# The last group's second channel product: one outer product moved to the end and left untransposed

## The chip, the cores and the metric

One core of a Trainium2 chip runs the kernel. The metric is the device time of one execution in microseconds (us). A profiled execution also gives a trace with a span, from the first to the last instruction. The engines are named as in the profile: PE is TensorE's matmul, PEld its weight load, DVE VectorE, ACT ScalarE, POOL GpSimd, SP the engine that issues most DMAs.

## The reference

Linear attention without softmax for 8 batches and 8 heads, and then an MLP mixer on its output. All is fp32.

```
kv  = einsum('bhsd,bhse->bhde', k, v);  o = einsum('bhsd,bhde->bhse', q, kv)
x   = o / sqrt(mean(o*o) + 1e-6) * g_norm          # to (8, 576, 512)
u   = x + transpose(relu(transpose(x) @ w_tok1) @ w_tok2)
out = u + relu(u @ w_ch1) @ w_ch2                  # w_ch1 512x1536, w_ch2 1536x512
```

The change is in the last line, in the product with `w_ch2` and in the addition to `u`.

## The kernel before

**Stages.** Until about 226 us the kernel computes attention and token mixing and writes `u` to `out` in DRAM. Then come the channel products, for nine units of 512 rows: the first 512 rows of each of the 8 batches, and the last 64 rows of all of them together. Group 0 is one unit; groups 1 to 4 have two units each.

**A channel product of two levels.** In groups 1 to 4 the product is split by a scheme with seven multiplications where a plain 2x2 block product has eight, and each of the seven is split so once more. So the first channel product of a group (`channel1`, L971) has seven outer products of seven inner products, and the second (`channel2`, L1028) as many. An inner product is three matmuls of 128x128 weights with 256 columns, each of which the trace lists as two records. Groups 1 to 4 thus have 98 inner products each.

**Places.** The order is written by hand. Each inner product has a place, and `beside[place]` lists the steps of the other engines that are recorded right behind it (`put`, L867). At the end one loop goes over the places, and so each engine's queue has this order. `outer` (L870) sets the seven inner products of one outer product to the places of `PLACE` (L863): 1, 5, (4 of the outer before), 6, 2, 3, 7, and its own 4 stands two places into the next outer. The very last outer uses `LAST` (L864), so that its 4 is in the last place: 1, 5, (4 of the outer before), 6, 2, 7, 3, 4. In the text "place p" of a channel product counts from its first inner product, so outer i starts at place 7i, and the last place of the last group is 49.

**What an inner product leaves.** The results are in three kinds of PSUM tiles: `ps_a` and `ps_b`, of which there is one each, and `ps_d`, of which there are two. Product 1 goes to `ps_a`, and ACT copies it to `ps_d`, where 6, 7 and 4 are added; 2 is added in `ps_a`; 5 goes to `ps_b`, and 3 is added there. After 5 and 6 a temporary is read (`p5`, `u2`; `read`, L885), and after 2, 3, 7 and 4 a quarter of the result is written. A quarter without `base` is read by an ACT copy (for 2 and 4) or a DVE add with `p5` or `u2` (`join`, L929, for 3 and 7); with `base` all of these reads are DVE adds.

**The second channel product.** The outer order is `ORDER2` (L949): 1, 2, 4, 7, 6, 5, 3. The left operands are sums of blocks of relu(u @ w_ch1), made by DVE: the wide sums of 128x1536 (`A`, `S1` to `S4`) and, for each outer, four steps of 128x768 to the tiles `sv` (`inner`, L1060; `ins[o][0]` to `ins[o][3]`). The weights of an inner product come from DRAM by SP, about seven to twelve places ahead (`fetch_ahead`, L963). The result is transposed by matmul order: weights `w` are stationary and the activations stream. Each result tile `rs[o]` is 128x1024, that is 128 columns by 512 rows of the output.

The four output quarters are: (0,0) = r1 + r2; (1,0) = r4 + r7 + r6 (r6 read with `base` r1); (1,1) = r7 + r5; (0,1) = r5 + r6 + r3, in running sums. The first index is the unit, the second the half of the output columns. A finished quarter is transposed in 32x32 blocks by DVE and added to `u` in DRAM by four accumulating DMAs from POOL (`put_rows`, L1173). In the last group (0,1) is taken another way: `xg`, loaded with `u` of that quarter and transposed ahead, gets r6 and r5, then outer 3's quarters straight from PSUM (`onto`), and is transposed back and stored in pieces (`store_part`, L1178), four stores of 32 KB each from SP, ACT and POOL:

```
(47, [store_part((nc.scalar, nc.sync), 0, (0,))]),
(48, [store_part((nc.sync, nc.scalar), 1, (1,)),
      store_part((nc.gpsimd, nc.sync, nc.gpsimd, nc.scalar), 0, (1,))]),
(49, [store_part((nc.sync, nc.scalar), 1, (0,))])
```

Of the kernel before, what the change touches and what calls it, by code (L numbers as in the profile page):

```python
# [20 lines left out]
def kernel(  # L21
# [33 lines left out]
    P = 128  # L55
# [64 lines left out]
    def dma(o, i, engine=nc.sync):  # L120
        keep(engine.dma_start(o, i))
# [7 lines left out]
    def copy(o, a):  # L129
        keep(nc.scalar.copy(o, a))  # L130

    def matmul(*a, **kw):
        keep(nc.tensor.matmul(*a, **kw))  # L133
# [462 lines left out]
    def units(g):  # L596
        return ((0,), (1, 2), (3, 4), (5, B), (6, 7))[g] if g < NG else (NU, NU)
# [272 lines left out]
    def outer(place, size, mul, to, base=None, act=copy, onto=False, last=False):  # L870

        banks, t = {}, {}
        places = LAST if last else PLACE

        def fit(flat):
            return flat.rearrange("p (n j) -> p n j", j=Q) if size == T else flat.rearrange("p (w t) -> p w t", w=W)
# [60 lines left out]
        put(place + places[7], do(join, 1, 1, "d", "p5"))  # L937
# [12 lines left out]
    order = [(w, g, o) for g in range(1, NG) for w, os in ((1, ORDER1), (2, ORDER2)) for o in os]  # L950
    ws, v_in_parts = {}, {}

    def fetch_w(n, k):
# [74 lines left out]
    def channel2(g, n0):  # L1028
# [3 lines left out]
        def second(i, o):  # L1032
            n = n0 + i
            r = {}

            def mul(p, ps, start, stop):
                v = v_in_parts[g, o](p)
                w = w_part(n, p).rearrange("p (w e) -> p w e", w=W)
                for s in range(W):
                    matmul(ps, lhsT=w[:, s], rhs=v[:, s], start=(start and s == 0), stop=stop,  # L1040
                           skip_group_check=True)
# [12 lines left out]
            return r  # L1054

        rs = {}
        for i, o in enumerate(ORDER2):
            rs[o] = second(i, o)

        def inner(o):  # L1060
# [49 lines left out]
        A, S1, S2, S3, S4 = (halves(f) for f in (make_a21, sum1, sum2, sum3, sum4))  # L1110


        for place, steps in (
                (-3, [ins[1][0]]), (-1, [ins[1][1]]), (1, [ins[1][3]]), (2, [ins[1][2]]),
                (3, [ins[2][0]]), (5, [ins[2][1]]), (6, [ins[4][0]]), (7, [ins[2][2]]),
                (8, [A[0]]), (9, [A[1]]), (10, [ins[2][3]]), (11, [S3[0]]), (12, [S3[1]]),
                (13, [ins[4][1]]), (14, [ins[4][2]]), (15, [S2[0]]), (16, [ins[4][3]]), (17, [ins[7][0]]),
                (19, [ins[7][1]]), (21, [S2[1], ins[7][2]]), (23, [ins[7][3]]), (24, [S1[0]]),
                (25, [ins[6][0]]), (29, [S4[0]]), (27, [ins[6][1]]), (28, [S1[1]]), (30, [ins[6][3]]),
                (31, [ins[6][2]]), (32, [ins[5][0]]), (33, [ins[5][1]]),  # L1120
                (35, [ins[5][2]]), (36, [ins[5][3]]), (38, [S4[1]]), (39, [ins[3][0]]), (41, [ins[3][1]]),
                (43, [ins[3][2]]), (45, [ins[3][3]])):
            put(b + place, *steps)

        def join(i, j, o):
            return do(put_rows, units(g)[i], j, lambda: rs[o][0])
# [5 lines left out]

            return step

        for place, step in ((19, radd(2, 1)), (20, join(0, 0, 2)), (39, radd(7, 6)), (40, radd(4, 7)), (41, join(1, 0, 4))):
            put(b + place, step)
        if g < NG - 1:
            for place, step in ((46, radd(7, 5)), (47, radd(5, 6)), (48, join(1, 1, 7)), (52, radd(3, 5)),
                                (55, join(0, 1, 3))):
                put(b + place, step)  # L1140
            if g == NG - 2:
                put(b + 60, do(fetch_x, g + 1))
                put(b + 79, do(turn, lambda: xg[g + 1]))
        else:
            for place, steps in ((38, [xadd(6)]), (44, [radd(7, 5), join(1, 1, 7)]), (46, [xadd(5)]),
                                 (47, [store_part((nc.scalar, nc.sync), 0, (0,))]),
                                 (48, [store_part((nc.sync, nc.scalar), 1, (1,)),
                                       store_part((nc.gpsimd, nc.sync, nc.gpsimd, nc.scalar), 0, (1,))]),
                                 (49, [store_part((nc.sync, nc.scalar), 1, (0,))])):
                put(b + place, *steps)  # L1150

        for k, place in enumerate((6, 8, 12, 36)):
# [22 lines left out]
        for b, at, to in pieces(u, j):  # L1175
            keep(nc.gpsimd.dma_start(to, t()[ds(b * Q, Q), at].rearrange("p n l j -> p n (l j)"), accum_op=ALU.add))  # L1176

    def store_part(queues, i, leaves):  # L1178
        def step():
            lo = leaves[0] * Q  # L1180
            t = xg[NG - 1][:, ts(i, NQ), leaves[0]]
            turn(lambda: t)
            for b in range(NC):
                dma(out[units(NG - 1)[0], ts(i, T), ds(DH + b * HF + lo, Q)].rearrange("(n i) e -> i n e", i=Q),
                    t[ds(b * Q, Q)], queues[b % len(queues)])

        return step

# [181 lines left out]
    def turn_over():  # L1370
        w2s.close()
        late["vr"] = pool("vr", 1, "right")
        late["sv"] = pool("sv", 2, "right")
        late["s3"] = pool("s3", 1, "right")
        late["xg"] = pool("xg", 1, "right")
        late["r"] = pool("r", 3, "right")

    put(9, turn_over)
# [43 lines left out]
```

## Time and profile before

| what | us |
|---|---|
| three runs, median (lowest to highest) | 785.08 (784.42 to 785.74) |
| the profiled execution, its own time | 784.74 |
| its span | 782.9 |
| PE busy in the span | 762.9 (97%) |
| DVE busy | 643.2 (82%) |
| ACT busy | 271.5 (35%) |
| POOL busy | 113.6 (15%) |
| second channel product of the last group, place 0 | starts at 707.15 |
| its last inner product (place 49) | starts at 772.81 |

The rest of the profiled execution's time, 1.84 us, lies around the span. The profile gives a start and a length for each instruction; a matmul's end is modelled, so that pace on PE is read from start to start. "Idle before" names what an engine waited for. DMAs have an issue on their engine's queue (SPq, ACTq, POOL) and a landing; the profile gives the time between them. In the chain of waits, work is followed back from the last instruction, at each step to what released it.

### The profile page before, as it was taken

The page shows a single profiled execution, that of the slowest core. Times are in us where ns is not written, and L with a number is a line of the kernel's source. Part 1 is how long each engine was busy: PE and PEld are TensorE (multiplying, and loading weights), DVE is VectorE, ACT ScalarE, POOL GpSimd, SP SyncE. Part 2 cuts the span into 40 slices and gives each one's busy share as a digit, 9 for nine tenths or more (in the row PEclk, how much of TensorE's full clock was granted, in tenths as well). Part 3 has the DMA queues.
Part 4 walks back from the last instruction along what each step waited for, and adds up shares of the span by engine and source line. Part 5 has one row for each costly group of instructions (what it writes and reads, how often), then busy time and mean ns, then how long its engine had stood idle before and what let it go on. Part 6 is the DMA issues. An engine that isn't in the chain of part 4 may idle for free.

```text
span 782.9 us, 12672 instructions
## 1 busy us (share of the span) xinstructions
PE 762.9 (97%) x4640; PEld 611.1 (78%) x4640; DVE 643.2 (82%) x957; ACT 271.5 (35%) x534; POOL 113.6 (15%) x130
## 2 busy tenths in 40 slices
PE   6999999999999999999999999999999999999994
PEld 6655555545888888888888888888888888888883
DVE  2867887897766779899978989987989996898995
ACT  2566575664210233511234241133351123424110
POOL 1002020113410000002240002051000236000205
PEclk9999999999999999999999999999999999999998
DMA  9999999999899796689997588899658889655658
GB/s 292 310 322 372 369 365 282 263 237 359 297 280 352 261 290 186 171 266 210 212 232 249 149 251 192 246 200 262 193 167 264 201 192 215 190 156 145 156 131 80
DMA packets 178412, 187.26 MB, mean 239 GB/s; under 512 B 76048, under 2 KB 141072, under 8 KB 178352
## 3 DMA queue, kind: packets, MB, share of 16 engines
q1 hardware_dynamic: 140208, 166.60, 70.4%
q0 software_dynamic: 34880, 18.42, 15.7%
q10 hardware_dynamic: 3264, 1.44, 0.7%
q8 instruction: 37, 0.61, 0.3%
q14 instruction: 23, 0.19, 0.1%
HBM read 137.79 MB, written 48.63 MB: 238 GB/s over the span
## 4 chain that ended last, share of the span: by engine, by line
PE 89%; DMA 5%; DVE 3%; POOL 1%; issue 0%; ACT 0%; ACTq 0%; POOLq 0%; SPq 0%; DVEq 0%
PE ps_d L133 26%; PE ps_b L133 18%; PE ps_a L133 17%; PE ps_u L133 8%; PE ps_h L133 7%; PE ps_v L133 5%; PE ps_c L133 3%; DMA v_in<-in_v_dram 2%; PE ps_w L133 2%; PE ps_kv L133 2%; PE ps_o L133 2%; DMA qR<-in_q_dram 1%; DVE v L124 1%; DMA k_in<-in_k_dram 1%; POOL out_dram L1176 1%; DVE sv L124 1%
## 5 line engine op out<-in xcount | busy, mean ns | idle before, releaser
L133 PE MATMUL ps_d<-ui,w 128*128 128x256 f32 x504 | 118.6, 379 | 0.0
L133 PEld LDWEIGHTS ps_d<-ui,w 128*128 128x128 f32 x504 | 95.8, 190 | 13.0
L130 ACT COPY ps_d<-ps_a 128x768 f32<-128x768 f32 (+1 forms) x56 | 32.0, 572 | 213.0 <-PE ps_a L133 210.0
L124 DVE TENSOR_TENSOR v<-v,v 128x1536 f32<-128x1536 f32 (+2 forms) x70 | 103.3, 1481 | 0.3
L1176 POOL DMA_DIRECT2D out_dram<-us x28 | 31.1, 1816 | 370.9 <-ACT p L130 366.0
L133 PE MATMUL ps_b<-sv,w 128*128 128x256 f32 x336 | 82.4, 381 | 1.4 <-DVE sv L124 1.0
L133 PE MATMUL ps_a<-v,w 128*128 128x256 f32 x336 | 81.7, 379 | 0.0
L133 PEld LDWEIGHTS ps_b<-sv,w 128*128 128x128 f32 x336 | 63.0, 190 | 12.9 <-DVE sv L124 2.8
L133 PEld LDWEIGHTS ps_a<-v,w 128*128 128x128 f32 x336 | 63.8, 190 | 8.7
L133 PE MATMUL ps_h<-x,w_tok 128*128 128x512 f32 (+1 forms) x160 | 65.2, 602 | 0.4 <-DVE x L503 0.4
L133 PE MATMUL ps_d<-v,w 128*128 128x256 f32 x264 | 64.3, 379 | 0.6 <-DVE xg L124 0.6
L133 PE MATMUL ps_u<-h,w_tok 128*128 128x512 f32 (+1 forms) x160 | 64.7, 599 | 0.0
L127 ACT ACTIVATE v<-v 128x768 f32<-128x768 f32 (+1 forms) x54 | 42.6, 822 | 55.1 <-DVE v L124 52.3
L133 PE MATMUL ps_d<-sv,w 128*128 128x256 f32 x240 | 58.3, 379 | 0.0
L1176 POOL DMA_DIRECT2D out_dram<-r x40 | 41.4, 1994 | 105.6 <-ACT p L130 81.6
L133 PEld LDWEIGHTS ps_d<-v,w 128*128 128x128 f32 x264 | 50.1, 190 | 7.7 <-DVE xg L124 1.0
L133 PEld LDWEIGHTS ps_h<-x,w_tok 128*128 128x128 f32 (+1 forms) x160 | 26.2, 189 | 32.0 <-issue 28.0
L133 PEld LDWEIGHTS ps_d<-sv,w 128*128 128x128 f32 x240 | 45.6, 190 | 6.2
L133 PEld LDWEIGHTS ps_u<-h,w_tok 128*128 128x128 f32 (+1 forms) x160 | 25.6, 179 | 31.1 <-issue 26.7
L133 PE MATMUL ps_a<-uT,w 128*128 128x256 f32 x192 | 46.7, 379 | 0.0
L133 PE MATMUL ps_b<-ui,w 128*128 128x256 f32 x168 | 40.8, 379 | 0.0
L133 PEld LDWEIGHTS ps_a<-uT,w 128*128 128x128 f32 x192 | 36.5, 190 | 5.0
(151 smaller groups left out, 1252.6 us busy)
## 6 DMA issues: line engine op xcount, KB each, us to landing
w<-parts SPq DMA_DIRECT2D x168, 384.0 KB, 3.7
w<-parts SPq DMA_DIRECT2D x56, 192.0 KB, 3.7
uT<-blocks SPq DMA_DIRECT2D x36, 256.0 KB, 5.2
k_in<-in_k_dram SPq DMA_DIRECT2D x16, 512.0 KB, 9.0
qT<-in_q_dram SPq DMA_DIRECT2D x8, 1024.0 KB, 9.7
out_dram<-x POOLq DMA_DIRECT2D x16, 512.0 KB, 6.3
v_in<-in_v_dram SPq DMA_DIRECT2D x14, 512.0 KB, 9.4
raw<-in_moe_w_ch_dram SPq DMA_DIRECT2D x8, 768.0 KB, 8.7
```

The lines of the kernel that those rows point to most:

```text
L124: keep(engine.tensor_tensor(out=o, in0=a, in1=b, op=op))
L127: keep(nc.scalar.activation(o, a, AF.Relu))
L130: keep(nc.scalar.copy(o, a))
L133: keep(nc.tensor.matmul(*a, **kw))
L1176: keep(nc.gpsimd.dma_start(to, t()[ds(b * Q, Q), at].rearrange("p n l j -> p n (l j)"), accum_op=ALU.add))
```

## The change

The outer product 2 of the last group's second channel product goes from second to last: the group's outer order becomes 1, 4, 7, 6, 5, 3, 2. Its operands are exchanged, activations stationary and weights streaming, so that its result has the output's rows on the partitions and needs no transpose; each inner product is then six matmuls of 128 columns in place of three of 256. Quarter (0,0) of the last group is put together in another way: r1 alone is copied by ACT to a new tile `xs` (`first_aside`), transposed, and added to `out` by `put_rows`; later the same rows are read back from `out` to `xs` untransposed (`fetch_last`, one DMA of 512 KB on SP, at place 34); outer 2 is added onto them from PSUM, and they are stored in four DMAs of 128 KB (`store_last`). Quarter (0,1) in `xg` is complete at place 44 and stored by a shorter `store_part`, in eight DMAs of 64 KB. The last group has its own list of places for the sums and the `sv` steps (`ends`).

In all groups outer 6 is now read without `base`; r1 is added afterwards in one DVE add of 128x1024 (`radd(6, 1)`, at place 38, in the last group at 31).

```diff
+    END = NG - 1, 2
+    order2 = lambda g: ORDER2 if g < NG - 1 else (1, 4, 7, 6, 5, 3, 2)
...
+                if (g, o) == END:
+                    for t in range(2):
+                        for s in range(W):
+                            matmul(ps[:, ts(t, P)], lhsT=v[:, s, ts(t, P)], rhs=w[:, s],
+                                   start=(start and t == 0 and s == 0), stop=stop, skip_group_check=True)
+                else:
+                    for s in range(W):
+                        matmul(ps, lhsT=w[:, s], rhs=v[:, s], start=(start and s == 0), stop=stop,
+                               skip_group_check=True)
...
-            if g == NG - 1 and o == 3:
-                outer(7 * n, T, mul, lambda i, j: xg[g][:, ts(i, NQ), j], onto=True, last=True)
-            else:
-                outer(7 * n, T, mul, to, o == 6 and (lambda i, j: rs[1][0][:, ts(i, NQ), j]))
+            if (g, o) == END:
+                outer(7 * n, T, mul, lambda i, j: rows_of(xs[0])[:, ts(i, 2), j], onto=True, last=True,
+                      fit=lambda flat: flat.rearrange("p (t b e) -> p t b e", t=2, b=NC))
+            elif g == NG - 1 and o == 3:
+                outer(7 * n, T, mul, lambda i, j: xg[g][:, ts(i, NQ), j], onto=True)
+            else:
+                outer(7 * n, T, mul, to)
...
+        ends = (
+                (-3, [ins[1][0]]), (-1, [ins[1][1]]), (1, [ins[1][3]]), (2, [ins[1][2]]),
+                (3, [A[0], ins[4][0]]), (5, [A[1]]), (6, [ins[4][1]]), (7, [S3[0]]), (8, [S3[1]]),
+                (9, [ins[4][3]]), (10, [ins[4][2], ins[7][0]]), (12, [ins[7][1]]), (14, [S2[0]]), (15, [ins[7][3]]),
+                (16, [ins[7][2]]), (17, [S2[1]]), (18, [ins[6][0]]), (19, [S1[0]]), (20, [ins[6][1]]), (21, [S4[0]]),
+                (22, [ins[6][3]]), (23, [ins[6][2]]), (24, [S1[1]]), (25, [ins[5][0]]), (26, [ins[5][1]]),
+                (27, [S4[1]]), (28, [ins[5][3]]), (29, [ins[5][2]]), (31, [ins[3][0]]), (32, [ins[3][1]]),
+                (33, [ins[3][3]]), (34, [ins[3][2]]), (36, [ins[2][0]]), (37, [ins[2][1]]), (39, [ins[2][2]]),
+                (40, [ins[2][3]]))
...
+        def first_aside():
+            xs[0] = late["xs"].tile([P, 2 * NQ, 2, Q], F32, name="xs")
+            copy(xs[0], rs[1][0])
...
+            for place, *steps in ((11, first_aside), (17, do(put_rows, units(g)[0], 0, lambda: xs[0])), (31, radd(6, 1)),
+                                  (32, radd(7, 6)), (34, fetch_last), (34, radd(4, 7)), (35, join(1, 0, 4)), (36, xadd(6)),
+                                  (38, radd(7, 5)), (39, join(1, 1, 7)), (41, xadd(5)),
+                                  (44, store_part(0)), (46, store_part(1)),
+                                  (48, store_last(0)), (49, store_last(1))):
...
+    def fetch_last():
+        xs[0] = late["xs"].tile([P, J, DH], F32, name="xs")
+        dma(xs[0], last_rows())
+
+    def store_last(i):
+
+        def step():
+            for t, queue in zip((2 * i, 2 * i + 1), (nc.sync, nc.scalar)):
+                dma(last_rows(t, 1), xs[0][:, ts(t, 1)], queue)
```

More of the change, by code (lines that the diff above doesn't have):

```diff
@@ L865, with outer @@
     products, beside = {}, defaultdict(list)
+    END = NG - 1, 2
     def put(place, *steps):
         beside[place] += steps
-    def outer(place, size, mul, to, base=None, act=copy, onto=False, last=False):
+    def outer(place, size, mul, to, base=None, act=copy, onto=False, last=False, fit=None):
         banks, t = {}, {}
         places = LAST if last else PLACE
-        def fit(flat):
-            return flat.rearrange("p (n j) -> p n j", j=Q) if size == T else flat.rearrange("p (w t) -> p w t", w=W)
+        fit = fit or (lambda flat: flat.rearrange("p (n j) -> p n j", j=Q) if size == T else
+                      flat.rearrange("p (w t) -> p w t", w=W))
         def bank(name):
@@ L949 @@
     ORDER1, ORDER2 = (1, 6, 2, 7, 5, 4, 3), (1, 2, 4, 7, 6, 5, 3)
-    order = [(w, g, o) for g in range(1, NG) for w, os in ((1, ORDER1), (2, ORDER2)) for o in os]
+    order2 = lambda g: ORDER2 if g < NG - 1 else (1, 4, 7, 6, 5, 3, 2)
+    order = [(w, g, o) for g in range(1, NG) for w, os in ((1, ORDER1), (2, order2(g))) for o in os]
     ws, v_in_parts = {}, {}
@@ L1038, in mul @@
                 w = w_part(n, p).rearrange("p (w e) -> p w e", w=W)
-                for s in range(W):
-                    matmul(ps, lhsT=w[:, s], rhs=v[:, s], start=(start and s == 0), stop=stop,
-                           skip_group_check=True)
+                if (g, o) == END:
[7 more added lines that the diff above has]
+                               skip_group_check=True)
             def to(i, j):
@@ L1056, in channel2 @@
         rs = {}
-        for i, o in enumerate(ORDER2):
+        for i, o in enumerate(order2(g)):
             rs[o] = second(i, o)
@@ L1110, in channel2 @@
         A, S1, S2, S3, S4 = (halves(f) for f in (make_a21, sum1, sum2, sum3, sum4))
-        for place, steps in (
+        usual = (
                 (-3, [ins[1][0]]), (-1, [ins[1][1]]), (1, [ins[1][3]]), (2, [ins[1][2]]),
@@ L1121, in channel2 @@
                 (35, [ins[5][2]]), (36, [ins[5][3]]), (38, [S4[1]]), (39, [ins[3][0]]), (41, [ins[3][1]]),
-                (43, [ins[3][2]]), (45, [ins[3][3]])):
+                (43, [ins[3][2]]), (45, [ins[3][3]]))
+        ends = (
[7 more added lines that the diff above has]
+                (40, [ins[2][3]]))
+        for place, steps in usual if g < NG - 1 else ends:
             put(b + place, *steps)
@@ L1133, in both @@
             return step
-        for place, step in ((19, radd(2, 1)), (20, join(0, 0, 2)), (39, radd(7, 6)), (40, radd(4, 7)), (41, join(1, 0, 4))):
-            put(b + place, step)
+        def first_aside():
+            xs[0] = late["xs"].tile([P, 2 * NQ, 2, Q], F32, name="xs")
+            copy(xs[0], rs[1][0])
         if g < NG - 1:
-            for place, step in ((46, radd(7, 5)), (47, radd(5, 6)), (48, join(1, 1, 7)), (52, radd(3, 5)),
-                                (55, join(0, 1, 3))):
-                put(b + place, step)
+            for place, *steps in ((19, radd(2, 1)), (20, join(0, 0, 2)), (38, radd(6, 1)), (39, radd(7, 6)), (40, radd(4, 7)),
+                                  (41, join(1, 0, 4)), (46, radd(7, 5)), (47, radd(5, 6)), (48, join(1, 1, 7)),
+                                  (52, radd(3, 5)), (55, join(0, 1, 3))):
+                put(b + place, *steps)
             if g == NG - 2:
@@ L1144, in channel2 @@
         else:
[L1145 to L1149, printed above, removed]
+            for place, *steps in ((11, first_aside), (17, do(put_rows, units(g)[0], 0, lambda: xs[0])), (31, radd(6, 1)),
[3 more added lines that the diff above has]
+                                  (48, store_last(0)), (49, store_last(1))):
                 put(b + place, *steps)
@@ L1176, in put_rows, with store_part @@
             keep(nc.gpsimd.dma_start(to, t()[ds(b * Q, Q), at].rearrange("p n l j -> p n (l j)"), accum_op=ALU.add))
[L1178 removed]
+    def store_part(i):
         def step():
[L1180 to L1181 removed]
+            t = xg[NG - 1][:, ts(i, NQ)]
             turn(lambda: t)
             for b in range(NC):
[L1184 to L1185 removed]
+                dma(out[units(NG - 1)[0], ts(i, T), ds(DH + b * HF, HF)].rearrange("(n i) e -> i n e", i=Q),
+                    t[ds(b * Q, Q)].rearrange("p n l j -> p n (l j)"), nc.scalar if i and b % 2 else nc.sync)
+        return step
+    last_rows = lambda t=0, n=J: out[units(NG - 1)[0], ds(t * P, n * P), :DH].rearrange("(t p) e -> p t e", p=P)
+    rows_of = lambda x: x.rearrange("p t (b l e) -> p t l b e", b=NC, l=2)
+    xs = {}
+    def fetch_last():
[5 more added lines that the diff above has]
+                dma(last_rows(t, 1), xs[0][:, ts(t, 1)], queue)
         return step
@@ L1375, in turn_over @@
         late["xg"] = pool("xg", 1, "right")
+        late["xs"] = pool("xs", 1, "right")
         late["r"] = pool("r", 3, "right")
```

## The prediction

> **What bounds the kernel now.** I read the page first (TensorE busy 97% of the span, DVE 82%, granted clock 0.996), then the chain of waits, then the timeline from 700 us on, and last the rows for single tiles. In the chain of waits the columns are start, length, what.
>
> ```profile
> 345.68 2.59 PE ps_d L133 x12
> 354.75 2.59 PE ps_d L133 x12
> 363.23 1.64 DVE v L124
> 365.20 1.66 DVE v L124
> 367.79 1.56 PE ps_b L133 x6
> 373.24 2.59 PE ps_d L133 x12
> ...
> 718.97 2.59 PE ps_d L133 x12
> 728.30 2.59 PE ps_d L133 x12
> 737.37 2.59 PE ps_d L133 x12
> ```
>
> An outer product (seven inner products, one "place" each) returns every 9.07 us: 1.295 us a place. Two intervals are longer. 354.75 to 373.24 is 18.49, where two periods make 18.13: 0.36 lost, at the ps_b product at 367.79 that waited for DVE. That is place 33 of the second channel product (3 of outer 6), and 482.29 to 500.78 and 609.83 to 628.32 show the same 0.36. 718.97 to 728.30 is 9.33: 0.26 lost at place 12 in the last group.
>
> ```profile
> 766.43 8.72 POOL L1176 DMA_DIRECT2D out_dram<-r  x8 [24.04 <-ACT r L130]
> 768.28 1.46 PE L133 MATMUL ps_d<-v,w 128*128 128x256 f32 x6
> 770.69 1.56 PE L133 MATMUL ps_b<-sv,w 128*128 128x256 f32 x6 [0.95 <-DVE sv L124]
> 772.81 1.56 PE L133 MATMUL ps_d<-v,w 128*128 128x256 f32 x6 [0.56 <-DVE xg L124]
> 773.14 5.50 SPq L121 DMA_DIRECT2D out_dram<-xg  x7
> 773.14 6.11 ACTq L121 DMA_DIRECT2D out_dram<-xg  x7
> 774.41 0.42 DVE L124 TENSOR_TENSOR xg<-ps_d,xg 128x256 f32<-128x256 f32 x1 [0.32 <-PE ps_d L133]
> ```
>
> From start to start the last two products come 770.69 - 769.575 = 1.115 and 772.81 - 771.985 = 0.825 us late: 1.94 us of DVE backlog. After the last product there are still 774.41 to 782.9 = 8.49 us:
>
> ```profile
> 774.40:782.90 8.50, 0.00 (x0) 0.00 (x0) 0.87 (x2) 0.00 (x0) 1.95 (x3) 0.66 0.95 105
> ```
>
> No engine works there; the DMA engines are 95% busy at only 105 GB/s, with sixteen 32 KB stores in rows of 128 B beside eight accumulating DMAs. The last store is issued at 778.94 and lands 2.6 us later; from that landing to the end of the span are 1.35 us.
>
> ```profile
> L121 ACTq DMA_DIRECT2D out_dram<-xg x1: 322/322/322, 778.9 to 778.9; - x1
> DMA to landing us min/median/max: 2.6/2.9/3.1
> ```
>
> So the end is set by TensorE's places, DVE's backlog on the last two, and a tail of small stores.
>
> **What the Trainium skill says.** "TensorE: Matmul & The Clock Gate", section "Back-to-back issue gap": the spacing of a stream of weight loads and matmuls is set by both, about 81 ns for bf16 with 128 columns, more than the columns alone would take. This kernel is fp32 and its trace has the shape itself, 112 ns (below), so the trace is used. "DMA: Bandwidth & Descriptors", section "Anatomy of one DMA — SWDGE (gpsimd) path": a DMA has about 2.0 us of fixed cost, mostly the write receipt. The trace agrees: 2.6 us for 32 KB, 2.8 us for 512 KB. The same page, "Specifications": below 512 B a row isn't moved at line rate. The trace agrees with 105 GB/s in the tail against 393 GB/s and more in slices around 260 us, where the rows are of 768 B to 3 KB.
>
> **The change part by part.**
>
> *a. Groups 1 to 3, outer 6 read without base.* Four DVE adds from PSUM (0.34 us each from start to start) become ACT copies (0.37; ACT is busy 35%), and one SBUF add of 128x1024 comes at place 38 (1.13 from start to start): DVE has 0.23 us less per group. What counts is that the p5 add (492.33 in group 2) stood in front of the sv that place 33 waits for. That sv ended at 495.28 and TensorE started at 495.33, when it could have at 493.78 + 1.295 = 495.075: 0.26 late, and 0.10 to refill. 0.33 us of relief covers this with 0.07 to spare. -0.36 x 3 = **-1.08**; bounds -1.1 and 0. The new add at 38 comes after more than it costs (1.36) has gone from the places before it.
>
> *b. Last group, place 12.* In the kernel before DVE came from the read at 715.19 to the sv for this product over four sv steps and two wide sums, and TensorE started at 722.88 in place of 722.69: 0.19 late and 0.07 to refill. In the new order there are two sv steps and three wide sums: 1.67 for 2 x 0.87 and 0.10 of a dependence, 0.17 sooner. It is a near thing: **-0.20**, bounds -0.26 and +0.1.
>
> *c. The untransposed product.* Each of the seven inner products of the last outer becomes six matmuls 128x128 in place of three 128x256: 12 records for 6. The nearest row is ps_o in the attention, also fp32, 128x128, with new weights for each matmul:
>
> ```profile
> 29.39 1.95 PE L133 MATMUL ps_o<-kvp,qT 128*128 128x128 f32 x16
> 31.18 1.88 PE L133 MATMUL ps_h<-x,w_tok 128*128 128x512 f32 x4
> L133 PEld LDWEIGHTS ps_o<-kvp,qT x56: 186/192/192, 18.9 to 34.5; 128*128 128x128 f32 x56
> ```
>
> (31.18 - 29.39) / 16 = 0.112 us a record, although a load is listed with 0.19: the loads overlap. 12 x 0.112 - 1.295 = 0.049, seven times: **+0.34**. Bounds: 0 (columns alone), and +7.1 if each load of 0.192 stood alone.
>
> *d. DVE's backlog.* The late steps (the last sv of outer 3, the wide add and the transposes between them) are no longer beside the last outer: outer 3's sv is made at places 31 to 34 and the last outer's at 36 to 40. Both late products lose their wait: -1.94. Another comes: place 43 (product 5 of the last outer) writes ps_b, of which there is one, and must wait for the DVE add that reads outer 3's join from it (place 40). From the last read that TensorE releases (outer 5's second join, place 34, readable 0.27 after its end) DVE has in a row: three PSUM reads of 256 (0.34), two SBUF adds of 256 (0.33), four sv steps of 768 (0.87), three adds of 1024 (1.13) and two transposes (1.16), 0.10 for one dependent pair and 0.08 for the last one's end: 1.02 + 0.66 + 3.48 + 3.39 + 2.32 + 0.18 = 11.05. TensorE gets from that release to place 43 in seven places less 0.27 plus one product of 1.344: 9.065 - 0.27 + 1.344 = 10.14. The wait is 0.91, with refill 1.0; bounds 0.4 and 2.5 (0.12 more for each of the thirteen steps). After it DVE has only six joins of 0.42, one add and two transposes for 9 us, so nothing is late again. -1.94 + 1.0 = **-0.94**.
>
> *e. The tail.* The column half that is transposed is now stored from places 44 and 46 in eight DMAs of 64 KB, rows of 256 B, about 6 and 3 us before the last product ends. The rest ends as: last product readable; one DVE add, 0.43; two DMAs of 128 KB in rows of 1 KB, one on SP and one on ACT, 0.03 to issue, 2.8 to land (the 512 KB store of group 0 took 2.8; the last pair is 256 KB, and I take no less because the pair before is still under way); 1.35 to close. 4.6 against 8.49: **-3.89**; the landing between 2.3 (192 KB of weights at 756.8) and 5.0 (POOL's stores of xg).
>
> *Queues.* The join of (0,0) moves from place 20 to 17, and the copy for it is 1 us on ACT. Its four DMAs on POOL were issued from 738.1 and landed by 747.3 (9.3 us); now about 731 to 741. The read-back is on SP behind the weights of place 33, at about 750, so SP finds them landed and the weights behind it (places 35 and 38, used at 47 and 49) aren't held. It is 512 KB; loads of that size took 9.0 us when crowded, so it is there by 759 for a first use at 766. The joins of (1,0) and (1,1) go to POOL at about 755 and 762 in place of 766 to 772; four take 9.3, so the last lands at 771.5, before the stores do. No cost.
>
> Sum: -1.08 - 0.20 + 0.34 - 0.94 - 3.89 = -5.77. The profiled execution took 784.74 (span 782.9 and 1.84 around it) and would take 779.0; the median of the three runs is 0.34 higher: 785.08 - 5.77 = **779.3 us**.
>
> **The rivals.**
>
> *The stores still drain.* The accumulates of (1,1), the xg stores and the xs stores meet between 767 and 775. If the last pair lands 2.3 us later (5.1, where POOL's stores of xg, issued at 774.4 and 775.0, took a median of 5.0), the time is 781.6. For it: small rows still fill the engines; a store waits for the landing of the eighth SP or ACT DMA before it, which can pass the delay on. Against: half as many packets as before, and started 5 us earlier. 0.12.
>
> *DVE later than summed.* Place 43 takes every delay of DVE one for one. If the wait is 2.5 us in place of 1.0, 780.8. For it: DVE is busy 96% from 761.8 to 774.4 (12.12 of 12.60). Against: such a sum over the sixteen DVE steps from 756.83 in the kernel before gives 13.85 us, so 770.68, and the sv for place 48 ended at 770.64. 0.12.
>
> *Slower: weight loads set the pace of the untransposed product.* 84 records at 0.192 are +7.1 in place of +0.34: 779.3 - 0.34 + 7.1 = 786.1. It decides from 0.112 + 5.77 / 84 = 0.181 us a record. For it: loads are listed with 0.19, twice as many for the same columns. Against: ps_o's 0.112. 0.05, and 0.04 for a slower case that I don't see in the new order.
>
> *It does not move the end*, because a store or POOL holds it as before: 784 to 785.5; 0.05.
>
> **How the numbers follow.** The forecast has 0.62 (own range 778.0 to 780.6), the stores 0.12, DVE 0.12, slower 0.09, unmoved 0.05. About 0.2% (1.6 us) is what a measurement can tell from no change. Faster takes the first three: 0.86; same 0.05; slower 0.09. The range 777.8 to 782.6 holds the first three with their bounds.
>
> **What would show it.** Right: no 18.49 intervals in groups 1 to 3; records of about 0.112 us in the last 9 us of TensorE; one wait of 0.7 to 1.0 us on DVE at place 43 and none at the last two; last landing about 3.3 us after the last product is readable. Wrong: records near 0.19; a wait on the read-back (DVE for xs) or on weights; DMA busy until well after the last store was issued.

## The result, and the profile after

| | before | after |
|---|---|---|
| median of 20 runs (lowest to highest), us | 785.51 (783.98 to 788.43) | 779.36 (777.15 to 784.99) |
| the profiled execution, us | 784.74 | 777.2 |
| its span, us | 782.9 | 775.4 |
| PE busy, us | 762.9 (97%) | 761.0 (98%) |
| DVE busy, us | 643.2 (82%) | 643.2 (83%) |
| second product of the last group, start of its last inner product to the end of the span, us | 10.09 | 5.30 |

The ratio of the times is 0.9934, with a 95% interval of 0.9916 to 0.9951: faster by more than this kernel's measurement needs to tell it from no change. The median is 0.06 us from the forecast of 779.3, which is closer than the working deserves (see the step by step account).

A single time is a poor measure here. Executions of the same kernel differ by several us in a stage that the change doesn't touch (last section), and so do the two spans shown: the same place of group 1, ahead of everything that was changed, starts at 345.68 before and at 344.65 after, so that 1.03 of the 7.5 us were there already. All that follows is read as intervals inside one trace, from this place on: 345.68 to 782.9 is 437.22 us before, 344.65 to 775.4 is 430.75 after. **6.47 us** is what there is to explain.

In the chain of waits of the kernel after (start, length, what), the lines that answer to those of before are:

```profile
344.65 2.59 PE ps_d L133 x12
353.71 2.59 PE ps_d L133 x12
...
366.67 1.35 PE ps_b L133 x6
371.90 2.59 PE ps_d L133 x12
...
717.00 2.59 PE ps_d L133 x12
...
726.24 2.59 PE ps_d L133 x12
```

353.71 to 371.90 is 18.19, where it was 18.49 and where two undisturbed periods make 18.13. The two DVE lines that stood in the chain ahead of place 33 are gone. Some 0.05 us is left: the `ps_b` product is listed with 1.35 us, where one that waits for nothing has 1.29. The same holds in groups 2 and 3 (18.18 each). In the last group 717.00 to 726.24 is 9.24, where it was 9.33.

The timeline of the kernel after, around its last outer product (in brackets the idle time ahead and what ended it):

```profile
759.74 1.53 PE L133 MATMUL ps_a<-w,v 128*128 128x128 f32 x12
...
762.00 1.60 PE L133 MATMUL ps_b<-w,sv 128*128 128x128 f32 x12 [0.72 <-DVE xg L124]
...
768.75 1.50 PE L133 MATMUL ps_b<-w,sv 128*128 128x128 f32 x12
770.10 1.50 PE L133 MATMUL ps_d<-w,v 128*128 128x128 f32 x12
...
771.63 0.42 DVE L124 TENSOR_TENSOR xs<-ps_d,xs 128x256 f32<-128x256 f32 x1 [0.91 <-PE ps_d L133]
```

768.75 to 770.10 is one of the new products: 1.35 us for twelve records, 0.112 each. Place 43 (762.00) comes 2.26 us after place 42, 0.92 more than a product takes, and the idle time names DVE's `xg`; the next product, at 763.44, adds 0.10 of refill (the pace behind a wait is a little slower for one product). The last two products wait for nothing; what waits now is DVE, 0.91 us for the last product to be readable. The row for ACT's last store of `xs`, and the time from issue to landing in the time behind this add:

```profile
L121 ACTq DMA_DIRECT2D out_dram<-xs x1: 377/377/377, 772.1 to 772.1; - x1
...
DMA to landing us min/median/max: 2.1/2.1/2.1
```

The last two stores, on SP and ACT, are issued 0.46 us after the start of the last add. ACT's lands 2.1 us later, and the span ends 1.2 us after that. In the stretch behind the last product (length; then busy time of PE, PEld, DVE, ACT and POOL; granted clock, DMA share, GB/s) the DMA engines are now busy for 42% of the time, where it was 95%:

```profile
771.60:775.40 3.80, 0.00 (x0) 0.00 (x0) 0.42 (x1) 0.00 (x0) 0.00 (x0) 0.85 0.42 138
```

### The profile page after: what moved, and what is told of

It is laid out like the page before. It is cut to its first block, busy times and chain, and to the rows that moved or that the text cites. A ratio compares the mean times of both kernels' runs of the same rounds, so it can differ in the third digit from the quotient of the medians.

```text
span 775.4 us, 12776 instructions
## 1 busy us (share of the span) xinstructions
PE 761.0 (98%) x4682; PEld 611.6 (79%) x4682; DVE 643.2 (83%) x946; ACT 277.4 (36%) x549; POOL 112.4 (14%) x128
## 4 chain that ended last, share of the span: by engine, by line
PE 94%; DVE 3%; DMA 1%; ACT 1%; issue 1%; SPq 0%; DVEq 0%; ACTq 0%
PE ps_d L133 27%; PE ps_b L133 19%; PE ps_a L133 18%; PE ps_u L133 8%; PE ps_h L133 8%; PE ps_v L133 5%; PE ps_c L133 3%; PE ps_o L133 2%; PE ps_kv L133 2%; PE ps_w L133 2%; DMA raw<-in_moe_w_tok_dram 1%; ACT x L499 1%; DVE r L124 0%; DVE sv L124 0%; DVE x L445 0%
## 5 line engine op out<-in xcount | busy, mean ns | idle before, releaser
L133 PE MATMUL ps_b<-sv,w 128*128 128x256 f32 x324 | 79.2, 380 | 0.1
L133 PE MATMUL ps_a<-v,w 128*128 128x256 f32 x324 | 78.8, 379 | 0.0
L1200 POOL DMA_DIRECT2D out_dram<-us x24 | 26.8, 1831 | 292.6 <-ACT p L130 287.3
L133 PEld LDWEIGHTS ps_b<-sv,w 128*128 128x128 f32 x324 | 60.8, 190 | 10.2 <-issue 2.1
L133 PEld LDWEIGHTS ps_a<-v,w 128*128 128x128 f32 x324 | 61.6, 190 | 8.4
L133 PE MATMUL ps_d<-v,w 128*128 128x256 f32 x258 | 62.7, 379 | 0.0
L133 PE MATMUL ps_d<-sv,w 128*128 128x256 f32 x228 | 55.4, 379 | 0.0
L133 PEld LDWEIGHTS ps_d<-sv,w 128*128 128x128 f32 x228 | 43.3, 190 | 5.9
```

## The experiments

Times of single profiled executions carry the spread of the early stage, so each is read from the trace: "from the common place" means from the line of two `ps_d` products that starts at 345.68 in the chain of the kernel before (345 to 351 in the others; these are places 16 and 17 of group 1's second channel product) to the end of the span, and "the tail" means from the start of the last product to the end of the span.

| kernel | common place to end | start of place 42 to start of 43 (last group) | tail |
|---|---|---|---|
| before | 437.22 | | 10.09 |
| after | 430.75 | 2.26 | 5.30 |
| after, once more (`after_again`) | 430.80 | 2.25 | 5.35 |
| e1 | 436.06 | | 9.86 |
| e2 | 430.59 | 2.26 | 5.37 |
| e3 | 436.69 | 1.34 | 11.61 |
| e4 | 434.43 | 2.26 | 8.98 |
| e5 | 429.77 | 1.33 | 5.34 |
| e7 | 429.32 | 1.34 | 5.43 |
| e8 | 431.52 | 2.26 | 6.08 |
| e9 | 433.99 | | 6.84 |
| e10 | 429.11 | 1.34 | 5.22 |

**e1: outer 6 without base, alone.** The kernel before, with this edit:

```diff
-                outer(7 * n, T, mul, to, o == 6 and (lambda i, j: rs[1][0][:, ts(i, NQ), j]))
+                outer(7 * n, T, mul, to, o == 6 and g == NG - 1 and (lambda i, j: rs[1][0][:, ts(i, NQ), j]))
...
+        if g < NG - 1:
+            put(b + 38, radd(6, 1))
```

> The kernel before with one part of the change alone: outer 6 is read without base, and r1 is added at place 38, in groups 1 to 3 (the last group stays as before). Theory (step a of the prediction: the p5 and u2 adds of outer 6 stood in front of the sv that place 33 waits for): the three intervals of 18.49 us shrink to 18.13 to 18.20, -0.9 to -1.1 us together, and the last group stays as it was: 9.33 at place 12, a wait of 0.95 and one of 0.56 us ahead of the last two products, about 10.1 us from the start of the last product to the end of the span. The span falls by about 1 us. Rival: the wide add at place 38 delays the adds behind it, so that a new wait of 0.2 to 0.4 us on DVE shows at places 40 to 47 of each group, and the sum stays within 0.3 us of before.

Its chain of waits in group 1:

```profile
355.20 2.59 PE ps_d L133 x12
...
368.15 1.34 PE ps_b L133 x6
373.38 2.59 PE ps_d L133 x12
382.45 2.59 PE ps_d L133 x12
```

355.20 to 373.38 is 18.18, and so in groups 2 and 3 (482.43 to 500.61, 609.66 to 627.84): 0.93 us in all. Behind place 38 the period is 9.07 again (373.38 to 382.45), so the wide add at 38 delays nothing. The last group keeps its 9.33, its two waits (0.96 and 0.56) and its long tail. The theory holds, and this part of the change is worth 0.9 us by itself; the other 0.2 us of 437.22 to 436.06 lie in the tail, which this edit doesn't touch.

**e2: the last outer without the exchange of operands.** The changed kernel, with its products as three matmuls of 256 columns; outer 2 is then added to quarter (0,0) of the last group in the transposed layout, so these sums are not those of the reference.

```diff
-                if (g, o) == END:
+                if False:
```

> The changed kernel without the exchange of operands: each of the seven products of the last outer is three matmuls of 256 columns with the weights stationary, as all others are. The sums of quarter (0,0) of the last group thus get outer 2 in the transposed layout, and are not those of the reference; everything else is left as it is. Theory (step c: twice the records, loads overlapped): the places of the last outer fall from 1.344 to about 1.295 us from start to start, so TensorE gains 0.05 us a product, 0.3 us over the last outer, and place 43 gets 0.05 us less time, so that its wait grows by 0.05. Rival (the weight loads are exposed somewhere in the last outer, in the first product or behind a wait): more than 0.6 us comes back.

```profile
764.10 1.49 PE L133 MATMUL ps_a<-v,w 128*128 128x256 f32 x6
...
766.36 1.56 PE L133 MATMUL ps_b<-sv,w 128*128 128x256 f32 x6 [0.77 <-DVE xg L124]
...
774.23 1.46 PE L133 MATMUL ps_d<-v,w 128*128 128x256 f32 x6
```

The last outer takes 10.13 us from the start of its first product to that of its last (764.10 to 774.23), where the changed kernel takes 10.36 (759.74 to 770.10). Six products at 0.05 less are 0.29, and the wait at place 43 is 0.05 longer (0.77 in place of 0.72): 0.24, and 0.23 is what is seen. Twice the weight loads cost 0.05 us a product and nothing else.

**e3: the sum of (1,1) moved back.** In the changed kernel:

```diff
-                                  (38, radd(7, 5)), (39, join(1, 1, 7)), (41, xadd(5)),
+                                  (41, xadd(5)), (45, radd(7, 5)), (46, join(1, 1, 7)),
```

> The changed kernel with the last group's sum of (1,1), its transpose and its four accumulating DMAs on POOL moved back from places 38 and 39 to 45 and 46, and xs without change at 41. Theory (step d: place 43 waits because 11 us of DVE work stand in a row from place 34 on): with 2.3 us of this row taken out the wait of 0.72 us at place 43 is gone and the last product starts about 1.0 us earlier. What it costs is a tail: POOL's four accumulates are issued at about 768 to 770 and land, at up to 8 us as before, at about 776 to 777, so that the span ends 0 to 2 us later than in the changed kernel (775.4). Rival 1: the wait comes from one late step and not from the row; then it stays at 0.6 us or more. Rival 2: the accumulates land in the 2 to 4 us that the SP and ACT stores take; then the span ends about 1 us earlier, at 774.4.

```profile
760.62 1.50 PE L133 MATMUL ps_a<-w,v 128*128 128x128 f32 x12
761.96 1.50 PE L133 MATMUL ps_b<-w,sv 128*128 128x128 f32 x12
...
770.19 4.36 POOL L1200 DMA_DIRECT2D out_dram<-r  x4 [9.79 <-issue]
...
770.59 1.60 PE L133 MATMUL ps_d<-w,v 128*128 128x128 f32 x12 [0.47 <-DVE xs L124]
```

In this timeline place 43 follows place 42 after 1.34 us: with 2.3 us of DVE work out of the row the wait is gone, as step d has it. But the work comes back at the end: the last product starts 1.97 us after the one before it (768.62), 0.63 late, on DVE. And the tail is 11.61 us, 6.3 more than in the changed kernel; from the common place to the end it is 5.9 us more, where 0 to 2 were expected. What SP waited for at the very end, how long the four accumulates took to land, and how long the last two stores did, is in the waits, in the rows for `r` and in those for `xs`:

```profile
SPq L1458 <- DMA out_dram<-r: 7.3, 1, 7.3
```

```profile
L1200 POOL DMA_DIRECT2D out_dram<-r x4: 1062/1741/2402, 770.2 to 772.1; - x4
...
DMA to landing us min/median/max: 6.1/8.1/8.3
```

```profile
DMA to landing us min/median/max: 5.9/5.9/6.0
```

The expectation had the accumulates issued by 770 and landed by 777. They were issued from 770.19 to 772.14, up to 2 us later, and took 6.1 to 8.3 us to land, where the same four take 3.2 to 6.0 in the changed kernel. The last landed at 780.4, and the span ended 1.8 us after it. Beside them the two last stores of `xs` took 5.9 us in place of 2.1. Rival 2 fell clearly, and so did rival 1.

**e4 and e8: the last stores cut up.** The changed kernel with the same bytes of `xs` in sixteen DMAs of 32 KB (e4), and in eight of 64 KB (e8), both in rows of 256 B in place of 1 KB:

```diff
-                dma(last_rows(t, 1), xs[0][:, ts(t, 1)], queue)
+                for b in range(NC):
+                    dma(last_rows(t, 1)[:, :, ts(b, HF)], xs[0][:, ts(t, 1), ts(b, HF)], queue)
```

```diff
-            for t, queue in zip((2 * i, 2 * i + 1), (nc.sync, nc.scalar)):
-                dma(last_rows(t, 1), xs[0][:, ts(t, 1)], queue)
+            for b in range(NC):
+                dma(last_rows(2 * i, 2)[:, :, ts(b, HF)], xs[0][:, ds(2 * i, 2), ts(b, HF)], (nc.sync, nc.scalar)[b % 2])
```

> The changed kernel with each of the four last stores of xs (128 KB, rows of 1 KB) cut into four DMAs of 32 KB with rows of 256 B: the same bytes, sixteen DMAs in place of four. Theory (step e: the tail was long because many small stores with short rows were issued late): from the start of the last product to the end of the span it takes 6.6 to 7.8 us in place of 5.3, of which about 0.3 us is the issue of eight DMAs on two queues after the last add and the rest later landing. Rival (lateness alone: the tail was long since the last DMA was issued 4.5 us after the last add, because of the DVE transposes between, and the size of rows matters little): 5.3 to 5.7 us.

> The changed kernel with the last xs stores in eight DMAs of 64 KB with rows of 256 B, so with the rows of e4 at half of its number of DMAs. From the start of the last product to the end of the span the changed kernel takes 5.3 us, and e4 took 9.0. Theory now (after e4, whose stores landed within 1.5 us each but were issued one after another, 0.48 us each, the last 4.2 us after the last add): the number of DMAs on a queue sets the tail and not the length of the rows; then 5.5 to 6.6 us, two more DMAs' worth of issue. Rival (short rows): 8 us or more, as in e4.

e4's tail was 8.98 us, above both expectations. Its rows for `xs` (duration of an issue, least, median and most in ns; first and last start):

```profile
L121 SPq DMA_DIRECT2D out_dram<-xs x8: 351/430/447, 774.3 to 777.7; - x8
...
DMA to landing us min/median/max: 1.5/1.6/1.7
```

The stores land faster than in the changed kernel, 1.6 us against 2.1 (they are a quarter of the size). What takes long is to get them issued: a queue issues one in about 0.48 us, so that ACT's eighth went out at 775.5, 2.0 us after the last add had ended. SP's eighth went out at 777.7, 4.2 us after it, and what held SP ahead of its first one is in its waits:

```profile
SPq L121 <- DMA out_dram<-xg: 2.4, 1, 2.4
SPq L121 <- DMA out_dram<-xs: 1.3, 2, 1.1
```

A store can wait until an earlier one has landed: SP waited 2.4 us so for its last store of `xg`, and 1.1 us for a landing of one of ACT's stores of `xs`. So e4's theory was right in the sign and wrong in the cause. e8 was made to tell the number of DMAs from the length of the rows. Its rows for `xs`:

```profile
L121 ACTq DMA_DIRECT2D out_dram<-xs x4: 378/422/508, 771.6 to 773.3; - x4
L121 SPq DMA_DIRECT2D out_dram<-xs x4: 375/432/498, 772.2 to 773.9; - x4
...
DMA to landing us min/median/max: 1.8/1.9/2.2
```

Its tail of 6.08 us lies in the range of the number: with rows of 256 B as in e4, but half as many DMAs, 2.9 of the 3.7 us are gone. The number counts twice, by the issues and by the landings that later stores wait for. The 0.8 us that are left hold both the four DMAs more and the shorter rows; no run changes the rows alone.

**e9: the kernel before without eight accumulates.** After e3 it was open what had made the tail of the kernel before long: its sixteen short stores, or the eight accumulates under way beside them. Here the last unit's accumulates are left out, so 512 rows of the output lack the channel product:

```diff
         turn(t)
+        if u == units(NG - 1)[1]:
+            return
         for b, at, to in pieces(u, j):
```

> The kernel before without the eight accumulating DMAs of the last unit (batch 7) on POOL: its two sums are made and transposed as before, but not added to the output, so 512 rows of the output lack the channel product. Everything else stays, the sixteen stores of xg in 128-B rows among it. The question is what made the tail of the kernel before long (10.1 us from the start of its last product to the end of the span). Theory (after e3: eight accumulates that are still under way slow every store and its issue, up to 1.2 us for one issue in place of 0.45): the issues on SP and ACT go back to about 0.5 us each, the last store is issued at about 3.5 us after the last product's start in place of 6.1, and the tail falls to 7 to 7.8 us. Rival (the sixteen short stores are enough by themselves): the tail stays at 9.3 us or more, and the issues still take 1 us and more.

The rows for `xg` in the tail, first of the kernel before, then of e9:

```profile
L121 SPq DMA_DIRECT2D out_dram<-xg x7: 338/463/1171, 773.1 to 778.3; - x7
L121 ACTq DMA_DIRECT2D out_dram<-xg x7: 322/499/1197, 773.1 to 778.9; - x7
```

```profile
L121 SPq DMA_DIRECT2D out_dram<-xg x7: 315/390/446, 778.2 to 781.2; - x7
L121 ACTq DMA_DIRECT2D out_dram<-xg x7: 322/408/470, 778.2 to 781.4; - x7
...
DMA to landing us min/median/max: 1.9/2.2/2.8
```

With the accumulates under way, single issues took up to 1.2 us and the last came 6.1 us after the start of the last product (772.81 to 778.94); without them no issue took over 0.5, and the last came after 3.5 (777.86 to 781.40). The tail falls from 10.09 to 6.84, a little under the range expected. So 3.25 of the 4.79 us that the change saves in the tail are had by taking the accumulates out of it alone. The other 1.54 are put down to what remains, fewer and longer stores behind the last product and no transpose there; no run splits them further. Rows of 128 B landed within 1.9 to 2.8 us, later than stores of the same 32 KB in rows of 256 B (1.5 to 1.7 us in e4), so short rows are not free; but with other stores under way beside them the two runs are no clean pair.

**e5 and e7: the wait at place 43 taken away without a late join.** e5 reads `ps_b` first:

```diff
-                (33, [ins[3][3]]), (34, [ins[3][2]]), (36, [ins[2][0]]), (37, [ins[2][1]]), (39, [ins[2][2]]),
-                (40, [ins[2][3]]))
+                (33, [ins[3][3]]), (34, [ins[3][2]]), (36, [ins[2][0]]), (37, [ins[2][1]]), (41, [ins[2][2]]),
+                (42, [ins[2][3]]))
...
-                                  (38, radd(7, 5)), (39, join(1, 1, 7)), (41, xadd(5)),
+                                  (40, radd(7, 5)), (40, join(1, 1, 7)), (41, xadd(5)),
```

> The changed kernel with one order of steps altered in the last group: the sum of (1,1) and its transpose are made at place 40, behind the DVE add that reads ps_b, in place of 38 and 39, and the last two sv steps one and two places later (41 and 42). No step is added or left out, and the accumulates on POOL go out about 3 us later than in the changed kernel, far from the place to which e3 moved them. Theory (step d: place 43 waits because the row of DVE work stands ahead of the one add that empties ps_b): that add comes 2.3 us earlier, the wait at place 43 is gone, and from the start of place 12's outer (726.24 in the changed kernel) to the start of the last product it takes 42.8 to 43.0 us in place of 43.86; no other wait above 0.2 us, and the tail stays 5.2 to 5.5 us. Rival 1 (DVE has no room to spare, as e3's new wait at the last product makes one think): the wait comes back at places 45 to 49, and 43.5 us or more stay. Rival 2 (the accumulates again fall into the tail): the tail is 6.5 us or longer.

e7 has this too, and in groups 1 to 3:

```diff
-                (8, [A[0]]), (9, [A[1]]), (10, [ins[2][3]]), (11, [S3[0]]), (12, [S3[1]]),
+                (8, [A[0]]), (9, [ins[2][3]]), (10, [A[1]]), (11, [S3[0]]), (12, [S3[1]]),
```

> e5 with a second exchange in groups 1 to 3: the last sv step of outer 2 at place 9 and the second wide sum A at place 10, in place of 10 and 9. In the changed kernel these groups still lose 0.26 us each at place 12, which waits for this sv (9.33 in place of 9.07). Theory (the same as for step b: what counts is what stands ahead of this sv in DVE's row, 1.7 us of a wide sum): the intervals of 9.33 become 9.07 in all three groups, 0.8 us together, so that with e5's 1.0 us it is 1.8 us faster than the changed kernel: a ratio to the kernel before of about 0.991. Rival: the sum A, one place later, is late for outer 4's first product (place 14), and 0.2 us or more a group shows there; then the gain is e5's alone, a ratio of 0.992.

> The changed kernel itself, beside e7 on the same chip and in the same rounds: a ratio to the kernel before of 0.9934, as before, or within 0.0015 of it; its trace again shows one wait of 0.7 us at place 43, 9.33 us at place 12 of groups 1 to 3, and 5.2 to 5.5 us from the start of the last product to the end of the span.

In e5's timeline place 43 (765.46) is on time; ahead of it is the line of its chain that the changed kernel has at 726.24:

```profile
730.62 2.59 PE ps_d L133 x12
```

```profile
764.13 1.50 PE L133 MATMUL ps_a<-w,v 128*128 128x128 f32 x12
765.46 1.50 PE L133 MATMUL ps_b<-w,sv 128*128 128x128 f32 x12
...
773.46 1.50 PE L133 MATMUL ps_d<-w,v 128*128 128x128 f32 x12
```

Nothing is late behind it: from 730.62 to the last product at 773.46 it is 42.84, against 43.86, so 1.02 us, with the tail as it was (5.34). Both rivals fell. One thing came otherwise than expected: the accumulates of (1,1) were not issued 3 us later, but 7.0 us ahead of the last product's start (766.42), where it had been 7.9. So e5 moved no load towards the tail, and says nothing of how late they may go.

In e7 the intervals of 9.33 in groups 1 to 3 are 9.07 as well, as group 1's shows, and the first products of the next outer wait for nothing:

```profile
336.41 2.59 PE ps_d L133 x12
...
345.48 2.59 PE ps_d L133 x12
```

`after_again` came as expected: 9.33 at this place, the wait of 0.72 at place 43, and a tail of 5.35. e7's median of six runs was 776.72 us, the changed kernel's beside it 779.7, that of before 784.8. The ratios to before are 0.990 (0.9875 to 0.9925) and 0.993 (0.9903 to 0.9957). These intervals overlap, so the times alone don't settle e7 against the changed kernel; the traces do: from the last such line ahead of group 1's place 12 to the end, e7 takes 438.39 us (336.41 to 774.8) and the changed kernel 440.08 and 440.13 in its two profiled executions. e7 is the better kernel by 1.7 us on the traces, where 1.8 were expected.

**e10: the stores of xg shared evenly.** e7 with

```diff
-                    t[ds(b * Q, Q)].rearrange("p n l j -> p n (l j)"), nc.scalar if i and b % 2 else nc.sync)
+                    t[ds(b * Q, Q)].rearrange("p n l j -> p n (l j)"), nc.scalar if i else nc.sync)
```

> e7 with the second half of the xg stores all on ACT: four on SP and four on ACT in place of six and two. In e7 SP waited for landings of its earlier stores and issued its last xs store 0.37 us after ACT's. Theory: both last xs stores are issued together, and from the start of the last product to the end of the span it takes 5.0 to 5.2 us in place of 5.43. Rival 1: ACT's four issues delay ACT's copies that the last outer needs, and the last product starts later (more than 42.9 us after the start at 726.53 in e7's trace). Rival 2: the landing of the last store sets the end, and the tail stays within 0.1 us.

```profile
770.13 1.69 SPq L121 DMA_DIRECT2D out_dram<-xs  x2
...
771.17 0.85 ACTq L121 DMA_DIRECT2D out_dram<-xs  x2
```

The start of the last product didn't move (42.84 again), so rival 1 fell. The tail was 5.22 in place of 5.43, a little short of the theory: the last store was now issued by ACT, at 771.62, because ACT had waited for the landing of a store of its own (770.99) and issued its first `xs` store only at 771.17. The traces of the changed kernel, of e5 and of e7 have tails of 5.30 to 5.43 with stores that are shared in the same way, so 0.2 us of one execution is a hint and not a result.

## Why the prediction was right, step by step

| step | predicted, us | measured, us | by |
|---|---|---|---|
| a, place 33 in groups 1 to 3 | -1.08 | -0.92 | three intervals of the chain, e1 |
| b, place 12 in the last group | -0.20 | -0.09 | 9.33 to 9.24 |
| c and d, untransposed product and DVE's backlog | +0.34 - 0.94 = -0.60 | -0.65 | places 16 and 17 to the last product, 44.51 to 43.86 |
| e, the tail | -3.89 | -4.79 | 10.09 to 5.30 |
| sum | -5.77 | -6.45 | of 6.47 |

The agreement of the median, 0.06 us, is luck in part. The steps sum to -5.77, 0.7 us less than the traces show. The two medians of 20 runs differ by 6.15, since they also carry the early stage (last section), and the forecast started from a median of three runs that lay 0.43 below that of twenty. These differences happen to cancel. What the prediction earns is each step's sign and, but for e and the near thing b, its size.

**a** was right in its mechanism: e1 shows that the adds ahead of this `sv` were the cause and that the moved add is free. In group 2:

```profile
492.44 1.46 PE L133 MATMUL ps_a<-v,w 128*128 128x256 f32 x6
492.65 0.95 DVE L124 TENSOR_TENSOR sv<-v,sv 128x768 f32<-128x768 f32 x1
...
493.67 1.16 PEld L133 LDWEIGHTS ps_b<-sv,w 128*128 128x128 f32 x6 [0.18 <-issue]
493.73 1.51 PE L133 MATMUL ps_b<-sv,w 128*128 128x256 f32 x6
495.07 1.46 PE L133 MATMUL ps_d<-v,w 128*128 128x256 f32 x6
```

The relief is what was summed: this `sv` ends 1.16 us after the start of the product ahead (493.60), where it was 1.50, and place 33 starts in time, 1.29 after that product. What the sum left out is 0.05 us inside place 33 itself (493.73 to 495.07 is 1.34). Its weight load starts only 0.06 us ahead of it, just after the `sv` is done, where loads otherwise start about 0.2 ahead; that this is the reason is argued from the times and was not tried. **b** was called a near thing and is one: place 12 starts 0.09 us sooner, where 0.17 was summed, and half of the gain came.

**c** is what `ps_o` had shown: 0.112 us a record, and e2 gives the price by taking it back. The slower rival, weight loads as the pace, needed 0.181 and fell. **d** met the wait at place 43: 0.91 and 0.10 of refill predicted, 0.92 and 0.10 seen. That the cause is the row of DVE work, and the one `ps_b` it must empty, is shown by e5, which changes nothing but the order and has the 1.0 us back. The rival of a longer DVE wait fell. The guess behind it was sound for another place: e3 shows that 2.3 us of DVE work at place 45 make the last product late.

**e** is the step with the largest error, -4.79 for -3.89. Two of its terms were mis-sized. The last stores were given 2.8 us to land, no less "because the pair before is still under way"; ACT's took 2.1, and the four stores took 1.7 to 2.1 in e5, e7 and e10, with the pair before under way in each. The close was given 1.35 us and took 1.2. That is 0.8 of the 0.9; the rest is the last product, which is readable 1.53 us after its start in place of 1.60.

The prediction also read the long tail of before as one of small stores with short rows, from 95% busy engines at 105 GB/s, and saw in this the statement of the Trainium skill ("DMA: Bandwidth & Descriptors", section "Specifications") that rows below 512 B aren't moved at line rate. The low rate was there, but it was not the main thing that made the tail long: e8 has rows of 256 B and a tail of 6.1 us, e9 the same sixteen stores in rows of 128 B as before and one of 6.8. The accumulates in flight made up 3.25 us of it (e9). For the rest, e4 and e8 speak for the number of stores in the changed kernel; in the kernel before it was not taken apart. The sum came out in spite of this reading, since the change moves the accumulates away, leaves fewer stores behind the last product and lengthens their rows, all at once. That the rows alone, made longer, would have brought little is argued from e8 and e9, not shown. The fixed cost of about 2.0 us that the prediction quotes is no floor for stores from SP and ACT: 32 KB landed in 1.5 to 1.7 us in e4.

**The queues** were free of cost, as said. The read-back was issued at 748.89, landed 5.2 us later and was first used at 764.32; the accumulates of (1,0) and (1,1) were issued from 755.19 and 762.19, and the last of them landed at 770.12, just as the last product started. That this is no small matter is what e3 shows. The rivals "the stores still drain" and "it does not move the end" both fell with the landing in 2.1 us.

## What to carry to other kernels

At the end of a kernel, first move the accumulating DMAs away from the last stores (3.3 of 10.1 us here), then issue few stores on each queue behind the last result: each more takes about 0.5 us to issue, and a later one may have to wait for its landing. The length of their rows mattered less in these runs, at most 0.8 us between 1 KB and 256 B (e8). Where an engine with one PSUM buffer waits, look which read empties the buffer and put that read ahead of the work that nobody waits for: it cost no instruction and brought 1.0 us. And compare intervals from a common place ahead of the change, before a difference of two total times is explained.

## What the runs showed that was not expected

**In the traces the spread comes from one early stage.** The two profiled executions of the changed kernel took 777.2 and 783.18 us, yet from the common place on they differ by 0.05 us. The difference lies around 140 to 160 us, in the attention and token mixing. The window 140 to 150 us, first of the shorter execution and then of the longer (after the length: busy time of PE, PEld, DVE, ACT and POOL; granted clock, DMA share, GB/s):

```profile
140.00:150.00 10.00, 9.41 (x115) 4.86 (x114) 8.46 (x18) 5.76 (x17) 1.43 (x2) 1.00 1.11 281
```

```profile
140.00:150.00 10.00, 6.12 (x104) 3.82 (x102) 5.02 (x12) 3.80 (x12) 0.74 (x1) 0.78 1.00 267
```

In the longer one PE idles for almost 4 of the 10 us, and the granted clock is 0.78 (and 0.88 in the 10 us after it). In all twelve traces the two go together: where PE was busy for 16.0 to 17.0 of the 20 us from 135 to 155, the clock there was 0.83 to 0.91 and the common place started at 349.0 to 350.7 (four traces); where it was busy for 18.4 us and more, the clock was 1.00 and the place started at 344.7 to 346.1 (eight). Which of the two brings the other was not tried.

**Accumulates slow other queues' DMAs.** One issue on SP or ACT took up to 1.2 us while POOL's eight accumulates were under way, and at most 0.47 without them (e9). With four under way no issue took over 0.5 (e3), so their number matters, or something else that goes with it; this was not tried. Four accumulates beside the last two stores of 128 KB stretched the landing of these from 2.1 to 5.9 us (e3).
